# Attention and two expert layers in one kernel: scores in quarters of TensorE's array, a new order around the second product and the end of routing, and weight loads queued behind gathers

## The chip, the cores and the metric

The kernel runs on one core of one Trainium2 chip. The core has a matrix engine (TensorE, in the profile PE, with its weight loads PEld), a vector engine (VectorE, DVE), a scalar engine (ScalarE, ACT), a general engine (GpSimd, POOL) and a queue engine (SyncE, SP). Each runs its own instructions in the order in which they are written; semaphores tie them together. Working memory is SBUF; TensorE writes only into the accumulator memory PSUM. Transfers (DMAs) are started from the queues of SP, ACT and POOL and share 16 DMA engines. The metric is the device time of one execution in microseconds (us); less is better.

## The reference

Three layers in float32, each feeding the next. The sizes are 2 batches, 8 heads, 768 positions, head size 64, so 1536 tokens of width 512.

```
scores = q @ k.T / 8 - slope[head] * distance     # kept: the first 8 keys, and the 96 last ones
a = softmax(scores);  x = a @ v                   # attention, tokens x 512
xn = x / rms(x) * rms_g
x2 = (silu(xn @ w_gate) * (xn @ w_val)) @ w_out   # 512 -> 1536 -> 512
skip = x2 @ w_skip > 0 ; e = argmax(x2 @ w_route) # 8 experts
out = x2 ; out[skip] += gate * relu(x2 @ w1[e]) @ w2[e]    # 512 -> 1024 -> 512
```

The numbers of global and local keys are inputs: the fast path serves up to 32 and 97, and a general attention stands behind a branch for all other values. It is not taken with the data at hand.

## The kernel before

The program is one hand-ordered stream (no scheduler moves anything). It has five stages.

**Start.** Constants are made, a flag is computed from the two numbers and read by all engines, and each engine branches over the general attention (L962, `with tc.If(flag == 0)`). That body is written out in full: for each of two heads of a pair, six blocks of 128 queries, on TensorE 216 matmuls and transposes in all. Behind it `bias_tiles` makes the additive bias in four instructions of 576 columns on VectorE (L109).

**Attention** runs over 24 items: 8 pairs of heads by 3 groups of 256 queries, one item a step and five items in flight. In a step TensorE does the scores of item t (`qk`, L222), the transposes of the softmax of item t-2 (`trans`, L268) and the products with v of item t-3 (`pv`, L293); VectorE adds the bias and takes the row minimum (`ttr`, L233), scales (`norm`, L260), copies one half of the transposes out of PSUM (L277) and makes half of the next layer's input (L395); ScalarE does the exponentials (`exp`, L244), the other copy (L279) and the rest of the input (L393, L394). For the scores q is laid out on the host with zeros: 128 rows by 1536 columns a pair, in which each block of 128 columns holds 64 queries of head 0 in the upper 64 rows and the same 64 queries of head 1 in the lower ones, so that one matmul with full rows and columns gives both heads. A matmul in float32 shows as two matmuls in the trace, so the 4 of a step show as 8, and the 8 of `pv` (64 columns of the array each) as 16.

**First product** (`gemm1`, L517): 12 blocks of hidden units, the operands split into a high and a low float32r part, three matmuls for each product.

**Second product** (`gemm2`, L583): 12 tiles t of 128 tokens, 36 matmuls of 512 columns each. After the last one ScalarE scales the result into `x2` (L587). Inside tile t, at hooks (column, k): `turn(t-1)` at (0, 1) transposes x2 of the tile before on TensorE and copies it on ScalarE into `x2t` (L560); `routed(t-1)` at (0, 4) makes the routing logits from `x2t` (L568) and the expert choice; `slots(t-2)` at (0, 9) collects token numbers. Behind gemm2(t) stand `split_h(t+2)`, which makes the high and low parts of a coming tile in six casts on ScalarE (L546) and six subtractions on VectorE (L547), then some splits of expert weights (`split_next`, after tiles 1, 2, 5 and 6: 3, 2, 2 and 1 chunks; a cast on ScalarE, L824, and a subtraction on VectorE, L833, for each chunk of 512 KB), then loads (`load_next`: 4 after tile 6, 5 after tile 9, and 4 more inside tile 11).

**End of routing and experts.** The first expert's input x0 is gathered with selection matmuls (L1180) while the last tile's logits, ranks (L1223, L1224) and choice are made in turn between TensorE, ScalarE and VectorE. Then expert 0's first matmul group runs (`up`, L871), in it `gathers` computes the token lists and starts four indirect DMAs on POOL (L848), then `tx(1)` (transposes of expert 1's rows, L858), `th(0)` (transposes of the hidden layer, L890), and the loop over 9 jobs: `up`, `th`, `down` (L903), `put`. The 72 chunks of expert weights come in a fixed order, and a loaded chunk takes the place ("slot") of something used up, so the order in which slots come free sets when loads start.

```
        (0, 1): lambda: t >= 1 and turn(s, t - 1),
        (0, 4): lambda: t >= 1 and routed(t - 1),
        (0, 9): lambda: t >= 2 and slots(s, t - 2)})
    if t + 2 < 12:
        split_h(s, t + 2)
```

## Time and profile before

| | |
|---|---|
| median of 3 runs (lowest, highest) | 573.92 us (572.85, 575.16) |
| profiled execution, its own time | 574.41 us |
| its span, first to last instruction | 572.7 us |
| TensorE matmul busy | 532.6 us, 93% |
| VectorE, ScalarE, GpSimd busy | 401.0, 277.7, 135.0 us (70%, 48%, 24%) |
| mean granted TensorE clock | 0.981 |
| moved by DMA | 83.79 MB, mean 146 GB/s |

How to read it: the shares are means over five stages with different limits, so windows of the span are read stage by stage. A busy TensorE in a window says only that matmuls were in flight, since their ends are modelled; the distance between the starts of two groups is the safer measure. A row of the timeline is "start us, us, engine line operation out<-in xcount", and a bracket at its end is the idle time of the engine just before it with what ended it. PEldq, DVEq and so on are the engines' sequencers, which take branches and semaphores.

### The profile page before, as it was taken

What the parts mean: (1) busy time and instruction counts of PE and PEld (TensorE: products, weight loads), DVE (VectorE), ACT (ScalarE), POOL (GpSimd) and SP (SyncE); (2) the same over time, 40 slices, a digit from 0 to 9 for tenths busy, and PEclk for the clock granted to TensorE, in tenths of its full rate; (3) what the DMA queues carried; (4) which work ended last, traced back from release to release, by engine and by line L of the source; (5) the groups of instructions that cost most, each with busy time, mean ns of one, the idle gap of its engine ahead of it and who ended that gap; (6) DMA issues with size and microseconds to landing.
All of it is one profiled execution on the core that took longest, in us unless ns stands there. A gap on an engine that the chain in (4) does not pass through costs nothing. (4 is left out here: it accounts for less than half of the span.)

```text
span 572.7 us, 8709 instructions
## 1 busy us (share of the span) xinstructions
PE 532.6 (93%) x2932; PEld 444.9 (78%) x2932; DVE 401.0 (70%) x1014; ACT 277.7 (48%) x630; POOL 135.0 (24%) x132
## 2 busy tenths in 40 slices
PE   1899998899999999999999988989998799999994
PEld 1788887788888888888888867867888587878883
DVE  2888989557888688768864255545442299999971
ACT  0689889224323333323323444335231196988850
POOL 1445556011222222222212000000000201566201
PEclk9899999899999999999999988999999899999998
DMA  8645521021223323333206211106066899999000
GB/s 300 263 180 223 196 89 39 1 75 61 96 102 110 111 80 105 110 112 110 102 10 224 106 41 66 42 37 221 37 251 220 266 340 330 367 396 367 32 15 17
DMA packets 29511, 83.79 MB, mean 146 GB/s; under 512 B 3512, under 2 KB 3640, under 8 KB 29457
## 3 DMA queue, kind: packets, MB, share of 16 engines
q1 hardware_dynamic: 26064, 75.95, 36.7%
q0 software_dynamic: 1520, 4.03, 2.1%
q10 hardware_dynamic: 1872, 3.15, 1.5%
q8 instruction: 26, 0.43, 0.3%
q14 instruction: 29, 0.23, 0.1%
HBM read 75.42 MB, written 8.65 MB: 147 GB/s over the span
## 5 line engine op out<-in xcount | busy, mean ns | idle before, releaser
L517 PE MATMUL ps<-xh,wh 128*128 128x512 f32 (+1 forms) x304 | 115.9, 381 | 0.1
L517 PE MATMUL ps<-xh,wl 128*128 128x512 f32 (+1 forms) x304 | 115.3, 379 | 0.4 <-POOL wl L483 0.4
L517 PE MATMUL ps<-xl,wh 128*128 128x512 f32 (+1 forms) x304 | 115.2, 379 | 0.0
L833 DVE TENSOR_TENSOR ewl<-eraw,ewh 128x1024 fp32r<-128x1024 f32 x72 | 83.7, 1231 | 1.9 <-ACT ewh L824 1.7
L824 ACT CAST ewh<-eraw 128x1024 fp32r<-128x1024 f32 x72 | 71.3, 1057 | 7.0 <-DVE ewl L833 6.7
L517 PEld LDWEIGHTS ps<-xh,wl 128*128 128x128 f32 x304 | 57.3, 189 | 11.7 <-POOL wl L483 0.9
L517 PEld LDWEIGHTS ps<-xh,wh 128*128 128x128 f32 x304 | 57.4, 189 | 11.2 <-issue 0.8
L517 PEld LDWEIGHTS ps<-xl,wh 128*128 128x128 f32 x304 | 57.5, 189 | 10.6
L470 DVE SCALAR_TENSOR_TENSOR wraw<-f64t,wraw 128x512 f32<-128x512 f32 x36 | 44.0, 1221 | 28.8 <-ACT f64t L468 28.8
L583 PE MATMUL px<-woh,hh 128*128 128x512 f32 (+1 forms) x156 | 62.8, 403 | 0.0
L547 DVE TENSOR_TENSOR hl<-h,hh 128x256 fp32r<-128x256 f32 x72 | 25.5, 423 | 50.7 <-ACT hh L546 50.7
L583 PE MATMUL px<-wol,hh 128*128 128x512 f32 (+1 forms) x156 | 59.7, 383 | 0.0
L583 PE MATMUL px<-woh,hl 128*128 128x512 f32 (+1 forms) x156 | 59.6, 382 | 0.0
L483 POOL TENSOR_TENSOR wl<-f64t,wh 128x512 fp32r<-128x512 f32 x24 | 31.0, 1292 | 101.4 <-ACT wh L482 58.1
L222 PE MATMUL sc<-kd,qd 128*128 128x192 f32 (+1 forms) x192 | 39.0, 353 | 12.3 <-DVEq L962 12.3
L244 ACT ACTIVATE es<-es,m 128x192 f32<-128x192 f32 (+1 forms) x96 | 41.5, 435 | 17.3 <-DVE m L233 16.3
L482 ACT CAST wh<-f64t 128x512 fp32r<-128x512 f32 x24 | 14.9, 621 | 71.4 <-DVE f64t L480 71.4
L260 POOL TENSOR_SCALAR es<-es,z 128x192 f32<-128x192 f32 x46 | 35.6, 784 | 43.6 <-DVE z L253 17.4
L222 PEld LDWEIGHTS sc<-kd,qd 128*128 128x128 f32 x192 | 32.9, 211 | 15.2 <-PEq L962 12.3
L583 PEld LDWEIGHTS px<-woh,hl 128*128 128x128 f32 x156 | 30.2, 193 | 5.8
L583 PEld LDWEIGHTS px<-woh,hh 128*128 128x128 f32 x156 | 30.1, 193 | 5.3
L583 PEld LDWEIGHTS px<-wol,hh 128*128 128x128 f32 x156 | 30.2, 194 | 4.2
(192 smaller groups left out, 974.2 us busy)
## 6 DMA issues: line engine op xcount, KB each, us to landing
eraw<-in_w_dram SPq DMA_DIRECT2D x72, 512.0 KB, 6.5
wraw<-in_wgv_dram SPq DMA_DIRECT2D x24, 512.0 KB, 3.7
wraw<-in_w_out_dram SPq DMA_DIRECT2D x12, 512.0 KB, 3.2
vp<-in_vx_dram SPq DMA_DIRECT2D x8, 704.0 KB, 5.0
qd<-in_qx_dram SPq DMA_DIRECT2D x7, 768.0 KB, 5.6
kd<-in_kx_dram SPq DMA_DIRECT2D x7, 464.0 KB, 6.6
xm<-x SPq DMA_DIRECT2D x12, 256.0 KB, 2.6
out_dram<-x ACTq DMA_DIRECT2D x12, 256.0 KB, 2.9
```

The lines of the kernel that those rows point to most:

```text
L222: nc.tensor.matmul(sc[r][:, x, 0:n], lhsT=qs[pr][:, 2 * (2 * g + r) + x, :], rhs=ks[pr][:, k0:k0 + n], start=True, stop=True)
L244: nc.scalar.activation(e[:, r, x, e0:e0 + n], e[:, r, x, e0:e0 + n], AF.Exp, bias=m[:, j:j + 1], scale=-1.0, accum_out=z[:, j:j + 1])
L260: eng.tensor_scalar(e[:, r, x, e0:e0 + n], e[:, r, x, e0:e0 + n], z[:, j:j + 1], None, ALU.mult)
L470: nc.vector.scalar_tensor_tensor(out=a.bitcast(F32), in0=t, scalar=F64_LEAST, in1=a.bitcast(F32), op0=ALU.is_ge, op1=ALU.mult)
L482: nc.scalar.copy(hi, t)
L483: eng.tensor_tensor(lo, t, f(hi), ALU.subtract)
L517: nc.tensor.matmul(p, lhsT=w[:, k, :], rhs=x[c][:, k, a:b], start=n == 0, stop=n == 11)
L547: nc.vector.tensor_tensor(hl[:, i, :], src, f(hh[:, i, :]), ALU.subtract)
L583: nc.tensor.matmul(p, lhsT=h[:, k, :], rhs=w[k][:, c:c + N], start=n == 0, stop=n == 35)
L824: eng.copy(wh, raw)
L833: eng.tensor_tensor(wl, raw, f(wh), ALU.subtract)
```

## The change

**Scores.** q is no longer padded: 128 rows (64 of each head) by 768 columns a pair. A step's 4 score matmuls become 8, each with 64 rows and 64 columns of the array, in the order (head, chunk) = (0,0), (1,1), (0,1), (1,0). The chunk decides the PSUM tile, and for odd chunks the heads change halves, so that the slopes of the bias exist in two orders and each of the four bias instructions becomes four (16 in all, of 64 to 192 columns). `pv` reads its operand in a matching order. On TensorE, one step before (scores of one item, transposes, products; the two `sc` tiles are the PSUM tiles of the two blocks of 128 queries):

```order
L222 MATMUL sc_924<-kd,qd 128x192 x2
L222 MATMUL sc_925<-kd,qd 128x192 x2
L268 MATMUL pt<-ident,es_799 128x128 x8
L293 MATMUL po<-pts,vp 64x128 x8
L222 MATMUL sc_981<-kd,qd 128x192 x2
```

and the same step now (the two `sc` tiles are those of the two chunks):

```order
L240 MATMUL sc_518<-kd,qd 64x192
L240 MATMUL sc_519<-kd,qd 64x192 x2
L240 MATMUL sc_518<-kd,qd 64x192 x2
L240 MATMUL sc_519<-kd,qd 64x192 x2
L240 MATMUL sc_518<-kd,qd 64x192
L286 MATMUL pt<-ident,es_368 128x128 x8
L313 MATMUL po<-pts,vp 64x128 x8
```

Twice as many score matmuls stand in a step, each with half the rows and half the columns; the rest of the step is as it was.

**General attention** (not executed) runs its six blocks in a loop, so that the code over which the first branch leads is shorter: on VectorE 212 listed instructions before and 66 now, on TensorE 216 matmuls and transposes before and 36 now.

**Second product.** `split_h(t+1)` moves into the hook (0, 1), behind `turn(t-1)`; routing moves from (0, 4) to (0, 5), and the splits of expert weights and their loads follow it there, one tile later than before. On ScalarE, from the result of tile 1 to that of tile 2, before:

```order
L587 ACTIVATE x_3904<-px,r_1722 128x512
L590 DMA out_dram<-x_3904 128x512
L546 CAST hh<-h_795 128x256
L546 CAST hh<-h_2356 128x256
L546 CAST hh<-h_2357 128x256
L546 CAST hh<-h_2358 128x256
L546 CAST hh<-h_2359 128x256
L546 CAST hh<-h_2360 128x256
L824 CAST ewh<-eraw 128x1024 x3
L560 COPY x2t<-pxt 128x512
L656 ACTIVATE rex,rz<-lg,rm 128x8
L587 ACTIVATE x_4012<-px,r_1722 128x512
```

and now:

```order
L608 ACTIVATE x_3564<-px,r_1376 128x512
L611 DMA out_dram<-x_3564 128x512
L581 COPY x2t<-pxt 128x512
L567 CAST hh<-h_364 128x256
L567 CAST hh<-h_2030 128x256
L567 CAST hh<-h_2031 128x256
L567 CAST hh<-h_2032 128x256
L567 CAST hh<-h_2033 128x256
L567 CAST hh<-h_2034 128x256
L677 ACTIVATE rex,rz<-lg,rm 128x8
L845 CAST ewh<-eraw 128x1024 x3
L608 ACTIVATE x_3660<-px,r_1376 128x512
```

The copy `x2t`, for which the logits wait, goes from behind six casts and three weight casts to their front; the weight casts now stand ahead of the next result.

**End of routing.** Dummy matmuls (`keep`, into a PSUM tile `idle` that nobody reads) stand between the dependent steps; selection and gates of tile 10 move into tile 11; x0 is cast in two halves; expert 0's `th` goes ahead of expert 1's `tx`; the exponentials and ranks of tile 11 go behind the cast of x0. The loads of tile 11 are gone: 6 loads stand in tile 10 (5 after tile 9 before), and 8 are started from POOL's queue behind the four gathers. On POOL, before:

```order
L619 MEMSET ones_3824 128x128
L1134 MEMSET early 128x512
L1193 DMA early<-xm,si_f 128x512
L848 DMA exg<-xm,gi_s 128x512 x4
L913 DMA out_dram<-eo,si_s 1536x512
```

and now:

```order
L1222 DMA early<-xm,si_f 128x512
L869 DMA exg<-xm,gi_s 128x512 x4
L837 DMA eraw<-in_w_dram 128x2x512 x2
L837 DMA eraw<-in_w_dram 128x1024 x4
L837 DMA eraw<-in_w_dram 128x2x512 x2
L936 DMA out_dram<-eo,si_s 1536x512
```

Eight loads of 512 KB stand between the gathers and the first scatter of results, on a queue that had none of them.

```diff
@@ bias_tiles
+    spans = [(0, 64, 0), (64, 192, 4), (192, 384, 0), (384, 576, 4)]
     for hp in range(4):
-        nc.vector.scalar_tensor_tensor(out=s.bias[:, hp, :], in0=rel, scalar=slopes[:, hp:hp + 1],
-                                       in1=miss, op0=ALU.mult, op1=ALU.add)
+        for a, b, z in spans:
+            nc.vector.scalar_tensor_tensor(out=s.bias[:, hp, a:b], in0=rel[:, a:b],
+                                           scalar=slopes[:, z + hp:z + hp + 1],
+                                           in1=miss[:, a:b], op0=ALU.mult, op1=ALU.add)
@@ general_attention
-                for i in range(6):
+                with tc.For_i(0, 6, 1) as i:
...
@@ attention: load
-        qs[pr] = ap.tile([128, 12, 128], F32, name="qd", bufs=3)
+        q = qs[pr] = ap.tile([128, 768], F32, name="qd", bufs=3)
-        for a, b, c, d in ((0, 512, 0, 288), (512, 1536, 288, 928)):
+        for a, b, c, d in ((0, 256, 0, 288), (256, 768, 288, 928)):
@@ attention: qk
-            for x in range(2):
+            for h, x in ((0, 0), (1, 1), (0, 1), (1, 0)):
                 k0, _, _, n = part(g, r, x)
-                nc.tensor.matmul(sc[r][:, x, 0:n], lhsT=qs[pr][:, 2 * (2 * g + r) + x, :],
-                                 rhs=ks[pr][:, k0:k0 + n], start=True, stop=True)
+                d = slice(64 * h, 64 * h + 64)
+                o = slice(64 * (h ^ x), 64 * (h ^ x) + 64)
+                i = 128 * (2 * g + r) + 64 * x
+                nc.tensor.matmul(sc[x][o, r, 0:n], lhsT=qs[pr][d, i:i + 64],
+                                 rhs=ks[pr][d, k0:k0 + n], start=True, stop=True)
@@ attention: pv
-                                 rhs=pts[:, kt, :, o], start=kt == 0 or i == 0, stop=kt == 1)
+                                 rhs=blocks[:, kt, hh:4 - hh:3 - 2 * hh, :],
+                                 start=kt == 0 or i == 0, stop=kt == 1)
@@ Expert.tx
-        nc.scalar.copy(self.xh, xt)
+        for k in ((0, 2), (2, 4)) if x0 else ((0, 4),):
+            nc.scalar.copy(self.xh[:, k[0]:k[1], :], xt[:, k[0]:k[1], :])
@@ the loop over gemm2
-        gemm2(s, t, {
-            (0, 1): lambda: t >= 1 and turn(s, t - 1),
-            (0, 4): lambda: t >= 1 and routed(t - 1),
-            (0, 9): lambda: t >= 2 and slots(s, t - 2)})
-        if t + 2 < 12:
-            split_h(s, t + 2)
-        if t in (1, 5, 9):
-            for q in range(6):
-                s.slots.add(early if t < 9 and q == 0 else big, [f"h{t // 4}{q}"])
-        split_next({1: 3, 2: 2, 5: 2, 6: 1}.get(t, 0))
-        load_next({6: 4, 9: 5}.get(t, 0))
+        def one():
+            if t >= 1:
+                turn(s, t - 1)
+                split_h(s, t + 1)
+            if t in (2, 6, 10):
+                for q in range(6):
+                    s.slots.add(early if t < 10 and q == 0 else big, [f"h{t // 4}{q}"])
+                load_next({6: 0, 10: 6}.get(t, 0))
+        def two():
+            if t >= 1:
+                routed(t - 1)
+            split_next({2: 3, 3: 2, 6: 2, 7: 1}.get(t, 0))
+            load_next({7: 4}.get(t, 0))
+        gemm2(s, t, {(0, 1): one, (0, 5): two, (0, 9): lambda: t >= 2 and slots(s, t - 2)})
@@ inside and behind gemm2(11)
     def tenth():
...
+        run(select(s, 10), gates(s, 10))
     def adds():
...
-        load_next(4)
+    def keep(n):
+        w = experts[0].w[0][0]
+        for _ in range(n):
+            nc.tensor.matmul(idle, lhsT=w[:, 0:128], rhs=w[:, 512:1024], start=True, stop=True)
...
     logits(s, 11, range(2))
-    add(s.x2[10], first[10])
+    keep(1)
     turn(s, 11, 1)
+    add(s.x2[10], first[10], range(2))
     logits(s, 11, range(2, 4))
+    add(s.x2[10], first[10], range(2, 4))
...
     nc.tensor.matmul(rk0, lhsT=s.ones16, rhs=s.cum[:, 11, 0:1], start=True, stop=False)
+    keep(2)
     nc.tensor.matmul(rk0, lhsT=s.tri, rhs=oh0, start=False, stop=True)
     choose(11, rk0, oh0)
+    keep(2)
+    add(s.x2[11], first[11], stop=True)
+    keep(3)
     run(rest)
-    exps(s, 11)
-    add(s.x2[11], first[11], stop=True)
     free_wo(3, 6)
-    ranks(s, 11, s.ps_m, "misc")
...
     experts[0].tx(x0)
-    run(select(s, 10), select(s, 11))
+    exps(s, 11)
+    ranks(s, 11, s.ps_m, "misc")
+    run(select(s, 11))
     def gathers():
...
         for e in (1, 0, 2, 3):
             experts[e].gather()
+        load_next(8, nc.gpsimd)
...
+    experts[0].th()
     experts[1].tx()
-    experts[0].th()
```

## Rows read from the trace of the kernel before

**Rows 1.** Busy time by stretch of the span: the stretch and its length, then busy us (and instructions) of PE, PEld, DVE, ACT and POOL, the granted TensorE clock, the DMA engines' share and GB/s.

```profile
40.00:60.00 20.00, 20.00 (x187) 17.74 (x184) 18.07 (x88) 18.39 (x68) 10.99 (x14) 1.00 0.54 203
...
80.00:100.00 20.00, 18.23 (x174) 15.55 (x171) 19.45 (x78) 18.96 (x68) 11.52 (x13) 1.00 0.08 28
...
480.00:500.00 20.00, 20.00 (x99) 16.48 (x98) 20.00 (x21) 17.48 (x24) 8.37 (x3) 1.00 0.95 338
```

**Rows 2.** The instructions of line 962, the first branch: engine, operation, count, duration in ns (least, median, most), first and last start in us.

```profile
L962 ACTq COMPARE_BRANCH  x1: 50/50/50, 5.6 to 5.6; - x1
...
L962 PEldq COMPARE_BRANCH  x1: 6047/6047/6047, 5.7 to 5.7; - x1
...
L962 DVEq EVENT_SEMAPHORE  x1: 21/21/21, 12.2 to 12.2; - x1
```

**Rows 3.** Timeline of the start, all engines.

```profile
2.20 0.43 SPq L203 DMA_DIRECT2D kd<-in_kx_dram  x1
...
6.27 0.19 POOL L103 CAST slopes<-rel 128x4 f32<-128x4 f16 x1 [4.57 <-POOLq L962]
...
12.31 6.73 PE L222 MATMUL sc<-kd,qd 128*128 128x64 f32 x24 [12.31 <-DVEq L962]
...
14.44 0.82 DVE L109 SCALAR_TENSOR_TENSOR bias<-rel,slopes,miss 128x576 f32<-128x576 f16 x1
15.41 0.23 DVE L233 CUSTOM_DVE_ANT_0 es<-sc,bias 128x64 f32<-128x64 f32 x1 [0.15 <-DVE bias L109]
```

**Rows 4.** DMA issues of the first 40 us: KB of each and median us from issue to landing, for the first piece of k.

```profile
kd<-in_kx_dram SPq DMA_DIRECT2D x1, 144.0 KB, 3.9
```

**Rows 5.** Timeline of PE in steady attention: a score group, what follows it, and the second product and score group three steps on.

```profile
30.41 1.57 PE L222 MATMUL sc<-kd,qd 128*128 128x192 f32 x8
31.81 0.82 PE L268 MATMUL pt<-ident,es 128*128 128x128 f32 x6
...
39.03 1.15 PE L293 MATMUL po<-pts,vp 128*64 128x128 f32 x16
40.10 1.57 PE L222 MATMUL sc<-kd,qd 128*128 128x192 f32 x8
```

**Rows 6.** Timeline of PE over the second product, its plain matmuls left out: the rank matmul that opens each of tiles 2 to 8, and the logits of tile 1.

```profile
327.60 0.18 PE L678 MATMUL rk<-cum,ones 128*128 128x8 bf16 x1
...
334.23 1.06 PE L568 MATMUL lg<-w9t,x2t 128*128 128x9 f32 x8 [2.44 <-ACT x2t L560]
...
341.75 0.18 PE L678 MATMUL rk<-cum,ones 128*128 128x8 bf16 x1
...
354.97 0.18 PE L678 MATMUL rk<-cum,ones 128*128 128x8 bf16 x1
...
364.82 0.18 PE L678 MATMUL rk<-cum,ones 128*128 128x8 bf16 x1
...
374.69 0.18 PE L678 MATMUL rk<-cum,ones 128*128 128x8 bf16 x1
...
386.31 0.18 PE L678 MATMUL rk<-cum,ones 128*128 128x8 bf16 x1
...
397.02 0.18 PE L678 MATMUL rk<-cum,ones 128*128 128x8 bf16 x1
```

**Rows 7.** Timeline of ACT in tile 2 of the second product.

```profile
328.92 1.94 ACT L546 CAST hh<-h 128x256 fp32r<-128x256 f32 x6 [0.43 <-ACT x L587]
330.76 2.94 ACT L824 CAST ewh<-eraw 128x1024 fp32r<-128x1024 f32 x3
333.60 0.57 ACT L560 COPY x2t<-pxt 128x512 f32<-128x512 f32 x1
```

**Rows 8.** Timeline of PE from the end of the second product to the second expert.

```profile
439.29 0.51 PE L568 MATMUL lg<-w9t,x2t 128*128 128x9 f32 x4
...
445.19 1.22 PE L871 MATMUL eph<-ewh,exh 128*128 128x512 f32 x2 [0.73 <-ACT exh L861]
...
448.73 0.71 PE L871 MATMUL eph<-ewh,exh 128*128 128x512 f32 x2
...
456.67 0.63 PE L858 MATMUL ext<-ident,exg 128*128 128x128 f32 x4 [3.20 <-DMA exg<-xm,gi_s]
...
458.33 0.73 PE L871 MATMUL eph<-ewh,exh 128*128 128x512 f32 x2
```

**Rows 9.** Busy time by stretch, columns as in rows 1, at the first expert's start.

```profile
444.00:448.00 4.00, 3.27 (x12) 2.18 (x11) 1.82 (x10) 0.83 (x3) 0.00 (x0) 0.59 0.48 164
```

**Rows 10.** Timeline of POOL: the first of the four gathers, and a gather in the loop over the experts.

```profile
449.85 1.00 POOL L848 DMA_INDIRECT exg<-xm,gi_s  x1 [17.47 <-DVE rz L665]
...
502.62 6.16 POOL L848 DMA_INDIRECT exg<-xm,gi_s  x1 [0.30 <-issue]
```

**Rows 11.** Timeline of DVE around that second gather: subtractions with two operands in SBUF (L833), and one that reads PSUM (L862).

```profile
502.12 5.77 DVE L833 TENSOR_TENSOR ewl<-eraw,ewh 128x1024 fp32r<-128x1024 f32 x5
507.79 0.70 DVE L862 TENSOR_TENSOR exl<-ext,exh 128x512 fp32r<-128x512 f32 x1
508.39 3.50 DVE L833 TENSOR_TENSOR ewl<-eraw,ewh 128x1024 fp32r<-128x1024 f32 x3
```

**Rows 12.** DMA issues from 430 to 470 us: median us from issue to landing of the four gathers, and of the earlier gather of tiles 0 to 8.

```profile
exg<-xm,gi_s POOLq DMA_INDIRECT x4, 7.7
early<-xm,si_f POOLq DMA_INDIRECT x1, 3.4
```

More of the change, by code (lines that the diff above doesn't have):

```diff
@@ L147, in general_attention @@
                     for j in range(6):
-                        nc.tensor.matmul(sc[:, j, :], lhsT=q[:, 128 * i:128 * i + 128],
-                                         rhs=k[:, 160 * j:160 * j + 128], start=True, stop=True)
+                        nc.tensor.matmul(sc[:, j, :], lhsT=qi, rhs=k[:, 160 * j:160 * j + 128],
+                                         start=True, stop=True)
                     t = p.tile([128, 768], F32, name="gt")
@@ L217, in qk @@
         pr, g = it
-        sc = [s.ps_g.tile([128, 2, 256], F32, name=f"sc{r}", tag=f"ps{r}", bufs=2) for r in range(2)]
+        sc = [s.ps_g.tile([128, 2, 256], F32, name=f"sc{x}", tag=f"ps{x}", bufs=2) for x in range(2)]
         for r in range(2):
-            for x in range(2):
+            for h, x in ((0, 0), (1, 1), (0, 1), (1, 0)):
                 k0, _, _, n = part(g, r, x)
-                nc.tensor.matmul(sc[r][:, x, 0:n], lhsT=qs[pr][:, 2 * (2 * g + r) + x, :],
-                                 rhs=ks[pr][:, k0:k0 + n], start=True, stop=True)
+                d = slice(64 * h, 64 * h + 64)
[3 more added lines that the diff above has]
+                                 rhs=ks[pr][d, k0:k0 + n], start=True, stop=True)
         m = ap.tile([128, 4], F32, name="m", bufs=4)
@@ L233, in ttr @@
         nc.vector.tensor_tensor_reduce(
-            out=e[:, r, x, e0:e0 + n], in0=sc[r][:, x, 0:n], in1=s.bias[:, pr % 4, b0:b0 + n],
+            out=e[:, r, x, e0:e0 + n], in0=sc[x][:, r, 0:n], in1=s.bias[:, pr % 4, b0:b0 + n],
             scale=-0.125, scalar=3.0e38, op0=ALU.add, op1=ALU.min,
@@ L283, in pv @@
         pts = outs.pop((it, r))[1]
+        blocks = pts.rearrange("p k x (h c) -> p k (x h) c", c=64)
         if r == 0:
@@ L627, in route @@
 def route(s, t):
-    V, p = s.nc.vector, s.hpool
+    V, p = s.nc.vector, s.ixpool if t == 11 else s.hpool
     lg, skip = s.lg[t][:, 0:8], s.lg[t][:, 8:9]
@@ L854, in tx @@
         s, nc = self.s, self.s.nc
-        if xt is None:
+        x0 = xt is not None
+        if not x0:
             xt = s.ps_e.tile([128, 4, 128], F32, name="ext", bufs=1)
@@ L951, in attn_moe_kernel @@
     ints = load_ints(s)
-    s.rel = s.apool.tile([128, 1156], F16, name="rel", bufs=1)
+    s.rel = s.apool.tile([128, 1160], F16, name="rel", bufs=1)
     s.keep = s.apool.tile([128, 576], F16, name="keep", bufs=1)
-    s.slopes = s.apool.tile([128, 4], F32, name="slopes", bufs=1)
+    s.slopes = s.apool.tile([128, 8], F32, name="slopes", bufs=1)
     nc.sync.dma_start(s.rel, rel)
@@ L1251, in gathers @@
             experts[e].gather()
+        load_next(8, nc.gpsimd)
     experts[0].up(gathers)
-    run(gates(s, 10), gates(s, 11))
+    run(gates(s, 11))
     experts[0].relu()
@@ L1257, in attn_moe_kernel @@
         slots(s, t)
-    slt2 = s.ixpool.tile([24, 256], F32, name="slt2", bufs=1)
+    slt2 = s.ixpool.tile([24, 256], F32, name="slt2", tag="early", bufs=1)
     nc.vector.tensor_tensor(slt2, slt, s.sl, ALU.add)
+    experts[0].th()
     experts[1].tx()
-    experts[0].th()
     tab = s.ps_m.tile([128, 2, 24], F32, name="tab", tag="misc", bufs=1)
@@ L1323, in layout @@
     B, H, S, D = q.shape
-    qT = q.transpose(0, 1, 3, 2).reshape(B * H // 2, 2, D, S // 64, 64)
-    qx = np.zeros((B * H // 2, 2, D, S // 64, 2, 64), q.dtype)
-    for h in range(2):
-        qx[:, h, :, :, h, :] = qT[:, h]
+    qx = q.transpose(0, 1, 3, 2).reshape(B * H // 2, 2 * D, S)
     kT = k.transpose(0, 1, 3, 2).reshape(B * H // 2, 2 * D, S)
@@ L1336, in layout @@
     vx = v[:, :, np.stack(rows, axis=1), :].reshape(B * H // 2, 2, 128, 11, D).transpose(0, 2, 1, 3, 4)
[L1337 removed]
+    return qx, kT[:, :, cols], vx
 def relative():
```

33 lines of the change are left out of this document (21 added, 12 removed).

## The prediction

> **What bounds the kernel now.** One core at a mean clock of 0.981 leaves nothing to compare between cores, and the chain of waits comes down to the last scatter, so I read the span stage by stage: first the busy time by stretch, then the timelines of the edited places. In steady attention TensorE fills 20.00 of 20 us, with ScalarE at 18.39 and VectorE at 18.07 just below it; from 80 us VectorE (19.45) and ScalarE (18.96) are ahead of TensorE (18.23); over the experts TensorE and VectorE are both at 20.00 [rows 1]. So shorter scores pay in early and middle attention only, and expert time is not shortened at all. What else can be gained are waits: at the first branch, in tiles 2 to 5 of the second product, and between the first and second expert. I go through these four terms. The profiled execution took 574.41 us, 0.5 above the median of 573.92; the sum is made against the first.
>
> **Term 1, the start.** ScalarE's branch takes 50 ns at 5.6 us and GpSimd works at 6.27, but TensorE's branch takes 6047 ns, to 11.75, and VectorE's semaphore behind its own comes at 12.2 [rows 2, 3]. All read the same flag, so the difference is in what follows the branch. The two late engines are those with the long jumped-over bodies (216 matmuls and transposes on TensorE); after the change 36 are left. I take it that the code behind a short body is there at once, and the two start at about 6.3. They can't start sooner: the first k piece is issued at 2.20 and needs 3.9 to land, 6.1 [rows 3, 4]. Scores start at 12.31 now, so 6.0 comes free. Against it stand the bias pieces. An instruction of 576 columns takes 0.82 us, one of 64 columns (another operation, the nearest) 0.23 [rows 3]: 1.15 ns a column and 0.16 fixed, so three more starts cost up to 0.48 for each of four pairs, 1.9 in all; from 0.4 if starts overlap as back-to-back rows do there. I take 0.8, since VectorE has a tenth of its time free in steady attention. Term 1: 6.0 - 0.8 = **5.2** (3.5 to 6).
>
> **Term 2, scores in quarters.** The score group of a full step starts at 30.41, the transposes behind it at 31.81: 1.40 us for 8 matmuls of 192 columns with the whole array, 175 ns each. The 16 of the second product, half the array wide, go from 39.03 to 40.10: 1.07, 67 ns each for 128 columns [rows 5]. There will be 16 score matmuls a step, each a quarter of the array. No row shows a quarter, so bounds: one after the other, 16 x 175 = 2.80; two at a time at the second product's rate per column (0.52 ns x 192 = 100 ns), 1.60; four at a time 2.80/4 = 0.70. I take 1.07, the row nearest in kind (16 small matmuls that share the array), which says that starts, not columns, set the pace. That frees 0.33 a step. A pair is three steps, 30.41 to 40.10, 9.69 us; TensorE would need 9.69 - 3 x 0.33 = 8.7, but ScalarE at 18.39 of 20 needs 0.92 x 9.69 = 8.9, and with the waits between them I take 9.0: 0.7 a pair. About five of the eight pairs are bounded by TensorE, the late ones by VectorE and ScalarE [rows 1]: 5 x 0.7 = **3.5**. Ends: 5 if ScalarE reaches its 8.9 in six pairs and the start of the pipeline is shorter too; a loss of 24 x 0.2 = 4.8, less what the late pairs hide (a third), so 3.3, if only two run at a time.
>
> A change of mode between matmuls costs nothing that these rows show apart. The Trainium skill, "TensorEngine Tiling (Array Packing)", section Key Properties, says that TensorE is drained when the tiling mode changes, which speaks against this edit: a step now has three modes in place of two. By the rule, with both of the step's changes inside the second product's 1.07 us, and 128 columns at the higher clock being 53 ns (16 of them 0.85), one change is at most 0.11 to 0.22 and 24 more cost up to 2.6 to 5 us, an estimate; the 3.5 would fall to about 0 and the time to 554, inside the forecast's own range. The trace agrees only so far as that 0.22 leaves room for it.
>
> **Term 3, the second product.** The rank matmul that opens the routing of a tile comes once a tile. Undisturbed tiles are 9.85 and 9.87 long (354.97 to 364.82 to 374.69). From 327.60 to 341.75 it is 14.15, then 13.22 to 354.97, later 11.62 (374.69 to 386.31) and 10.71 (to 397.02): 4.3 + 3.4 + 1.8 + 0.8 = 10.3 above 9.86 [rows 6]. These are the tiles with expert weight splits. The mechanism is in ScalarE's queue: six casts (1.94) and three weight casts (2.94) run ahead of the copy x2t, which starts at 333.60 only [rows 7], and TensorE stands 2.44 us for it before the logits [rows 6]. The change puts x2t ahead of both. The casts behind it, 1.94 + 2.94, end some 5 us into a tile of 9.86, before the next x2 is due, and the subtractions on VectorE have the rest of the tile. What is late next is the weight casts against the next x2: they stand ahead of it, and I give 0.5 for the tiles where they brush it. Term 3: 10.3 - 0.5 = **9.8** (8 to 10.3; at 8 if the first of these tiles keeps half of its excess).
>
> **Term 4, the end of routing.** Expert 0's first group starts at 445.19 with a wait of 0.73, its next part at 448.73, the second expert's transposes at 456.67 after 3.20 of waiting for a gather, its first group at 458.33: 13.1 us from one to the other [rows 8]. Three parts: (a) TensorE's clock is 0.59 from 444 to 448 [rows 9], after a chain of short steps with gaps; in those 4.0 us it does what 0.59 x 4.0 = 2.4 would do, 1.6 lost; the dummy matmuls are to fill the gaps. (b) The wait of 3.20: the gathers took 7.7 us to land, the earlier one 3.4 [rows 12], and no loads of tile 11 are queued with them now, while th(0) goes into that time. (c) The start moves up some 0.6 since exponentials and ranks leave the path. 1.6 + 3.2 + 0.6 = 5.4; I take **4.6**, since the loads that expert 0's used chunks set free can still meet the gathers (2 to 5.6). The dummies themselves cost at most the end of one that overhangs its gap, 0.3.
>
> The loads on GpSimd: eight issues behind the gathers. A gather's issue takes 1.00 with 0.3 between [rows 10], so 8 x 1.3 = 10.4 us in which the queue is taken. Queued behind them are the first scatter and the fifth gather; both are needed only a job later (about 12 us), which hides it. The bound from above is the issue of 6.16 at 502.62 [rows 10]. There VectorE ran subtractions with two SBUF operands to 507.79, then one that reads PSUM; the issue ended at 508.78, though SBUF subtractions went on from 508.39 [rows 11]. So it was its start, with the read of the list, that was held, and a load without a list need not be. From below it is 0 (the cover holds), from above 8 x 6.2 - 10.4 = 39 of queue, of which two jobs of about 12 hide 24. I take 0, by the 1.00 row. The Trainium skill, "SBUF — State Buffer", on which engines contend, says that VectorE with two SBUF inputs holds up GpSimd work that reads SBUF; plain loads would be free of it, which agrees with 0, and the 6.16 row agrees with the rule.
>
> **Sum.** 5.2 + 3.5 + 9.8 + 4.6 = 23.1; 574.4 - 23.1 = 551.3, and on the median's side 550.8: **551**.
>
> **Rivals.**
> *Quarters one after the other* (slower). If the four quarters don't overlap, a score group is 16 x 175 = 2.80, 1.40 more a step; TensorE becomes the bound in all 24: +33.6, against 5.2 + 9.8 + 4.6 = 19.6 gained elsewhere: 588. It turns slower from 1.40 + 19.6/24 = 2.22 a step, 139 ns a matmul. Against it: the 16 of the second product, half as wide, already run at 67 ns [rows 5]. 4%.
> *Quarters two at a time.* 1.60 a step, term 2 is -3.3 for 3.5: 558. For it: the rate per column is what the half-array rows show. 15%.
> *The start stays.* If the branch waits for something other than the length of the body (a fetch at any jump, say), the change doesn't do what it says: 551 + 5.2 + 0.8 = 557. For it: no row shows what the 6047 ns are. Against it: 50 ns on ScalarE at the same branch. 12%.
> *GpSimd's loads are held.* If every issue took 6.16, 39 - 24 = 15 of queue would lie bare, the later chunks would land late and TensorE wait for them in jobs 1 and 2; as only issues that begin beside such a subtraction are held, I price a third of it, 5: 556. 9%.
> *The stall of the second product moves* to the next x2: half of term 3 back, 556. 3%.
> Forecast 57%.
>
> **How the numbers follow.** The forecast's own range is 546 to 555 (about half of each term's width, since they are independent). The range runs from 545 to 560, which takes in each rival but the first. A measurement of this kernel can tell about 0.5%, 2.9 us, from no change. All cases but the first are faster by more: 94%, with 2% for several together ending within 0.5%, and 4% slower.
>
> **What would show it.** VectorE and TensorE at work by about 6.3 to 6.5; score groups of 16 in about 1.07 and pairs some 9.0 apart; the second product's tiles all near 9.86 with x2t right behind the transposes; first groups of experts 0 and 1 about 9 us apart at a granted clock near 1.0; GpSimd's load issues near 1 us. Wrong would make it: a score group over 1.4, a branch still at 6 us, waits for x in the second product, or waits for chunks in jobs 1 and 2.

## The result

The changed kernel takes **554.33 us** (median of 4 runs, 554.07 to 554.68) against 574.33 for the kernel before (median of 4): ratio 0.9657, 95% interval [0.9641, 0.9673], so 19 to 21 us less. The forecast was 551, with a range from 545 to 560.

The same places of the program can be read off both traces. A "lead" is how much sooner the changed kernel gets there; its growth is what the stretch between two places gave.

| place | before, us | after, us | lead | gained on the way | forecast |
|---|---|---|---|---|---|
| first score matmul | 12.31 | 6.77 | 5.54 | 5.54 | 6.0 (term 1, ahead of the bias) |
| sixth score group | 30.41 | 25.33 | 5.08 | -0.46 | -0.8 (term 1, the bias pieces) |
| last score group | 92.83 | 85.62 | 7.21 | 2.13 | 3.5 (term 2) |
| first product starts | 104.91 | 99.14 | 5.77 | -1.44 | 0 |
| its last matmul | 309.61 | 303.05 | 6.56 | 0.79 | 0 |
| tenth rank matmul | 426.60 | 410.18 | 16.42 | 9.86 | 9.8 (term 3) |
| first expert starts | 445.19 | 428.72 | 16.47 | 0.05 | 0.6 (term 4c) |
| its next part starts | 448.73 | 430.96 | 17.77 | 1.30 | 1.6 (term 4a) |
| second expert starts | 458.33 | 438.38 | 19.95 | 2.18 | 3.2 (term 4b) |
| last scatter starts | 566.38 | 545.91 | 20.47 | 0.52 | |

Three of four terms came within 0.6 of their forecast: the first with 5.08 for 5.2, the third with 9.86 for 9.8, the fourth with 4.05 in all for 4.6 (5.4 for its parts, of which 4.6 was taken). The second, for which the scores were put into quarters, gave 2.13 from the sixth to the last score group, and 1.44 of it was lost again behind the last one. The rows, in order of the program:

**Start.** The instructions of the first branch in the changed kernel (engine, operation, count, duration in ns least/median/most, first and last start), which answer to [rows 2]:

```profile
L985 ACTq COMPARE_BRANCH  x1: 50/50/50, 5.9 to 5.9; - x1
...
L985 PEldq COMPARE_BRANCH  x1: 227/227/227, 6.0 to 6.0; - x1
L985 DVEq COMPARE_BRANCH  x1: 67/67/67, 6.0 to 6.0; - x1
...
L985 DVEq EVENT_SEMAPHORE  x1: 21/21/21, 6.6 to 6.6; - x1
```

and VectorE's branch in the kernel before:

```profile
L962 DVEq COMPARE_BRANCH  x1: 67/67/67, 5.7 to 5.7; - x1
```

TensorE's branch fell from 6047 ns to 227. VectorE's own branch takes 67 ns, and it took 67 before the change too: VectorE had not been late at its branch. In both kernels its semaphore comes last, 0.3 to 0.4 us behind TensorE's (6.3 and 6.6; 11.8 and 12.2), so it stood there until TensorE came. The bias of a pair of heads takes 1.21 us in four pieces for 0.82 in one, and by the sixth score group the lead is down to 5.08.

**Steady attention.** Timeline of TensorE over one pair, as in [rows 5]:

```profile
30.64 0.88 PE L240 MATMUL sc<-kd,qd 64*64 64x192 f32 x16
31.45 1.19 PE L286 MATMUL pt<-ident,es 128*128 128x128 f32 x8
...
38.53 0.93 PE L313 MATMUL po<-pts,vp 128*64 128x128 f32 x12
39.38 0.88 PE L240 MATMUL sc<-kd,qd 64*64 64x192 f32 x16
```

A score group now takes 0.81 us to the next group (31.45 - 30.64), 51 ns a matmul: four at a time, near the bound of 0.70, better than the 1.07 taken. The pair takes 8.74 where 9.0 was forecast and 9.69 stood [rows 5]. So far the step is better than its forecast. The busy times by stretch (columns as in [rows 1]) show where this ends:

```profile
40.00:60.00 20.00, 18.08 (x239) 12.81 (x232) 19.37 (x87) 18.37 (x70) 12.86 (x14) 1.00 0.52 178
60.00:80.00 20.00, 18.03 (x223) 13.90 (x221) 18.59 (x92) 17.35 (x62) 9.36 (x11) 1.00 0.27 92
```

From 40 to 60 us VectorE is at 19.37 of 20, and TensorE at 18. The pair that starts at 48.12 takes to 58.10, 9.98 us, longer than the 9.69 of [rows 5]. And behind the last score group stands a drain. Timeline of TensorE at the end of attention in the changed kernel:

```profile
85.62 0.88 PE L240 MATMUL sc<-kd,qd 64*64 64x192 f32 x16
...
90.09 0.66 PE L286 MATMUL pt<-ident,es 128*128 128x128 f32 x4 [1.68 <-DVE pts L295]
91.22 0.63 PE L286 MATMUL pt<-ident,es 128*128 128x128 f32 x4 [0.47 <-ACT pts L297]
...
95.51 1.97 PE L286 MATMUL pt<-ident,es 128*128 128x128 f32 x8 [2.33 <-DVE pts L295]
97.41 1.80 PE L313 MATMUL po<-pts,vp 128*64 128x128 f32 x16
99.14 0.50 PE L538 MATMUL ps<-xh,wh 128*128 128x512 f32 x1
```

and the two ends of the same stretch in the kernel before:

```profile
92.83 1.57 PE L222 MATMUL sc<-kd,qd 128*128 128x192 f32 x8
...
102.11 1.09 PE L268 MATMUL pt<-ident,es 128*128 128x128 f32 x8 [2.81 <-DVE pts L277]
...
104.91 0.80 PE L517 MATMUL ps<-xh,wh 128*128 128x512 f32 x1
```

At the last score group the lead is 7.21; the drain takes 13.52 in place of 12.08, and 5.77 is left. TensorE waits in it for VectorE's copies (1.68 and 2.33; before, 0.57 and 2.81), and the last transposes take 1.97 for 1.09, at a granted clock of 0.57 (92 to 100 us).

**Second product.** ScalarE in the tile in which it had run nine casts ahead of x2t [rows 7], and the rank matmuls that open the routing of tiles (as in [rows 6]):

```profile
323.25 0.59 ACT L581 COPY x2t<-pxt 128x512 f32<-128x512 f32 x1 [1.33 <-PE pxt L580]
323.73 1.94 ACT L567 CAST hh<-h 128x256 fp32r<-128x256 f32 x6
...
328.40 2.93 ACT L845 CAST ewh<-eraw 128x1024 fp32r<-128x1024 f32 x3
331.24 0.68 ACT L608 ACTIVATE x<-px,r 128x512 f32<-128x512 f32 x1
```

```profile
321.04 0.18 PE L699 MATMUL rk<-cum,ones 128*128 128x8 bf16 x1
...
330.95 0.18 PE L699 MATMUL rk<-cum,ones 128*128 128x8 bf16 x1
...
340.86 0.18 PE L699 MATMUL rk<-cum,ones 128*128 128x8 bf16 x1
```

x2t comes first, the weight casts end at 331.3, just as the next result is due, and the tiles are 9.91 and 9.91 long; all nine up to 410.18 are between 9.89 and 9.91.

**End of routing.** Timeline of TensorE, as in [rows 8], then GpSimd's queue, as in [rows 10]:

```profile
428.72 0.71 PE L894 MATMUL eph<-ewh,exh 128*128 128x512 f32 x2
...
430.96 0.72 PE L894 MATMUL eph<-ewh,exh 128*128 128x512 f32 x2
...
435.85 1.14 PE L913 MATMUL eht<-ident,eh 128*128 128x128 f32 x8
437.05 0.66 PE L880 MATMUL ext<-ident,exg 128*128 128x128 f32 x4
...
438.38 0.73 PE L894 MATMUL eph<-ewh,exh 128*128 128x512 f32 x2 [0.45 <-ACT exh L884]
```

```profile
432.07 1.00 POOL L869 DMA_INDIRECT exg<-xm,gi_s  x1 [16.07 <-DVE rz L686]
...
437.00 3.17 POOL L837 DMA_DIRECT2D eraw<-in_w_dram  x5
442.03 0.54 POOL L837 DMA_DIRECT2D eraw<-in_w_dram  x1 [1.87 <-DMA exg<-xm,gi_s]
444.40 0.72 POOL L837 DMA_DIRECT2D eraw<-in_w_dram  x1 [1.83 <-DMA exg<-xm,gi_s]
```

From expert to expert it is 9.66 us for 13.14, 3.48 less, in two parts. The first matmuls, up to the expert's next part, take 2.24 for 3.54 [rows 8], at a granted clock of 1.00 where 0.59 stood [rows 9]: 1.30. The other 2.18 come behind them. The wait of 3.20 for the gather is gone: the second expert's transposes start 5.0 us after the first gather's issue, 6.8 before [rows 8, 10], and th(0) fills the time. The eight loads on GpSimd take 0.54 to 0.80 each; the last four are issued while VectorE runs its weight subtractions without a break (439.35 to 448.5).

### The profile page after: what moved, and what is told of

Its sections match the earlier page's. It is cut to its first block, busy times and chain, and to the rows that moved or that the text cites. A ratio compares the mean times of both kernels' runs of the same rounds, so it can differ in the third digit from the quotient of the medians.

```text
span 552.3 us, 9096 instructions
## 1 busy us (share of the span) xinstructions
PE 524.2 (95%) x3132; PEld 425.8 (77%) x3132; DVE 404.8 (73%) x1026; ACT 277.5 (50%) x631; POOL 140.8 (25%) x140
## 5 line engine op out<-in xcount | busy, mean ns | idle before, releaser
L604 PE MATMUL px<-wol,hh 128*128 128x512 f32 (+1 forms) x156 | 58.2, 373 | 0.0
L262 ACT ACTIVATE es<-es,m 128x192 f32<-128x192 f32 (+1 forms) x96 | 41.4, 434 | 11.5 <-DVE m L251 10.3
L286 PE MATMUL pt<-ident,es 128*128 128x128 f32 x176 | 30.5, 305 | 10.1 <-DVE pts L295 6.6
L286 PEld LDWEIGHTS pt<-ident,es 128*128 128x128 f32 x176 | 20.7, 152 | 21.6 <-DVE pts L295 10.0
```

Source lines behind the costliest of these rows:

```text
L262: nc.scalar.activation(e[:, r, x, e0:e0 + n], e[:, r, x, e0:e0 + n], AF.Exp, bias=m[:, j:j + 1], scale=-1.0, accum_out=z[:, j:j + 1])
L286: nc.tensor.transpose(pt[:, kt, x, :], e[:, r, x, 128 * kt:128 * kt + 128], s.ident)
L604: nc.tensor.matmul(p, lhsT=h[:, k, :], rhs=w[k][:, c:c + N], start=n == 0, stop=n == 35)
```

## Experiments

Each edit is shown against the kernel named. Times are medians; ratios are to the kernel before on the same chip. *Loop*, *quarters* and *second* do one part of the change alone.

**Loop.** The kernel before, with the blocks of the general attention in a loop.

```diff
-                for i in range(6):
+                with tc.For_i(0, 6, 1) as i:
```

> The kernel before with the six blocks of the general attention in a loop, nothing else. If the wait at the first branch hangs on the length of the body that is jumped over: the branch on TensorE ends by about 6.5 us in place of 11.75, first scores at 6.3 to 6.8, and the time falls by 5.5 to 6.3 (about 568.4). If the branch waits for something else (rival), it still takes about 6 us and the time stays within 1 us of the kernel before.

569.33, ratio 0.9903 [0.9881, 0.9926]: 4.3 to 6.8 us less. TensorE's branch takes 233 ns, scores start at 6.52. The first theory holds. How much of the start's 5.8 reaches the end differs from execution to execution: in the profiled one, the slowest of four (571.57), the lead is 4.84 at the first product and 2.73 at the first expert.

**Quarters.** The kernel before, with plain q, scores in quarters and 16 bias instructions (the parts of the change's diff for bias_tiles, load, qk and pv).

```diff
+            for h, x in ((0, 0), (1, 1), (0, 1), (1, 0)):
+                nc.tensor.matmul(sc[x][o, r, 0:n], lhsT=qs[pr][d, i:i + 64],
+                                 rhs=ks[pr][d, k0:k0 + n], start=True, stop=True)
```

> The kernel before with scores in quarters (plain q, 16 bias instructions) and nothing else. Theory V, that attention as a whole is bounded by VectorE, whose work grows by 1.6 us for the bias: the score group falls from 1.40 to about 0.8 us on TensorE, but the start of the first product moves by less than 1 us either way and the time stays within 1.5 us of the kernel before. Theory T, that TensorE bounds five of eight pairs as the prediction had it: the first product starts 3 to 4 us sooner and the time falls by 3 to 4.

573.25, ratio 0.9983 [0.9962, 1.0004], which is not clear of no change. The score group falls to 0.81 us. From the first score to the first product it is 92.10 us (12.91 to 105.01) against 92.60 before. Theory V's numbers came out, theory T's did not: 0.5 us from some 13 of matmul time saved (24 steps at 0.5 to 0.6). How sure is the 0.5? *Loop* and *second* have the attention of the kernel before, and take 93.55 and 91.84, so a single profile is good to about 1 us here. The stretch from the sixth to the last score group is steadier: 62.43, 62.42 and 62.43 in these three, 60.31 in this run, and 60.27 to 60.48 in the changed kernel, *nokeep*, *sploads*, *noswap* and *third*. Quarters bring 2.1 there, and the ends of attention take it back.

**Second.** The kernel before, with the new order around the second product.

```diff
-            (0, 4): lambda: t >= 1 and routed(t - 1),
+        gemm2(s, t, {(0, 1): one, (0, 5): two, (0, 9): lambda: t >= 2 and slots(s, t - 2)})
-        if t + 2 < 12:
-            split_h(s, t + 2)
```

> The kernel before with the new order around the second product alone (split_h, routing, weight splits and loads moved; 5 loads in tile 10, 4 in tile 11 as before). If x2t behind the casts was the whole cause of the long tiles: all tiles 9.85 to 9.95, the first expert starts 9.5 to 10 us sooner, the time falls by 9.5 to 10.5 (about 564.3). If part of the stall moves to the next x2 (rival): a tile over 10.5 remains and the time falls by 5 or less.

563.07, ratio 0.9799 [0.9779, 0.9820]: 10.3 to 12.7 less. All tiles are 9.84 to 9.87 long; from the end of the first product to the first expert it is 125.84 us, 135.58 before: 9.74. The first theory holds. The time fell somewhat more than the 9.74 of that stretch; the profiled execution was also 1.25 ahead when the first product ended, in a part of the program that the edit doesn't touch.

**Diagonal.** The changed kernel, without the swap of heads for odd chunks, so that only two of the four quarters are in use, and with four bias instructions.

```diff
-                o = slice(64 * (h ^ x), 64 * (h ^ x) + 64)
+                o = d
```

> The changed kernel, but with the heads not swapped for odd chunks: each head's scores stay in its own half of columns, so only the two diagonal quarters of the array are used, and the bias is again four instructions of 576 columns (1.6 us less for VectorE). Score group by the rate of the second product per column: 1.4 to 1.6 us against 0.81 of the changed kernel; if neighbours in one quarter run strictly one after the other, no two at once, 2.8. Theory V: the time stays within 1 us of the changed kernel (554.3), since TensorE has room for 0.6 a step and VectorE gets 1.6 back. Theory T: the time rises by 3 to 5.

557.56 (554.10 to 558.99), ratio 0.9687 [0.9639, 0.9734]: wide, and by time not apart from the changed kernel. The trace is plainer: a score group takes 1.45 us (90 ns a matmul, somewhat less than the 100 ns that the rate per column of the products with v gave for two at a time), a pair 9.89, and the first product starts at 103.28, 4.1 later than in the changed kernel. TensorE is busy for 20.00 of 20 us from 40 to 60 and from 60 to 80: it is the bound again, and theory T's numbers came out for this kernel. So neither theory is the whole: two at a time TensorE decides, four at a time it does not.

**Poolnorm.** The changed kernel, with one more scaling of a step on GpSimd.

```diff
-            norm(b, 0, 1, nc.vector)
+            norm(b, 0, 1, nc.gpsimd if t < n else nc.vector)
```

> The changed kernel, with one of the two remaining scalings by 1/z of a step moved from VectorE to GpSimd (24 instructions of 0.28 to 0.35 us off VectorE, 24 of 0.8 onto GpSimd, which is busy 10 to 13 of 20 us there). Theory V, that VectorE bounds attention as a whole now: pairs after the fifth become shorter, the first product starts 2 to 4 us sooner than at 99.14, the time is 550 to 552. Theory T, that the loss lies with TensorE's own tail and clock: no change within 1 us. Rival G: GpSimd, at some 2.4 of 2.95 us a step, becomes late itself and the step grows: 556 or more.

**550.14**, ratio 0.9576 [0.9556, 0.9596], clear of the changed kernel's interval. The first product starts 3.0 us sooner:

```profile
84.38 0.88 PE L240 MATMUL sc<-kd,qd 64*64 64x192 f32 x16
...
96.15 0.80 PE L538 MATMUL ps<-xh,wh 128*128 128x512 f32 x1
```

VectorE has some 7 us less to do (24 scalings of about 0.3), and TensorE's work is the same. Theory V's numbers came out, but not its place: the late pairs did not become shorter. From the sixth to the last score group it is 61.02 us for 60.30. TensorE still waits there for VectorE's copies (0.97 and 0.75), and now for GpSimd's scalings too (0.27 twice). The gain lies at the two ends: 16.55 for 18.56 up to the sixth score group, 11.77 for 13.52 behind the last.

**Oldnorm.** The same one-line edit on the kernel before.

> The kernel before with one scaling by 1/z of a step moved from VectorE to GpSimd and nothing else. If TensorE bounds the steps of the kernel before (as the prediction had it): the spacing of its score groups stays at 9.7 a pair and the first product starts less than 1.5 us sooner. If VectorE bounded attention there already: the first product starts some 3 us sooner, as it did when the same edit was made to the changed kernel.

569.44, ratio 0.9928 [0.9903, 0.9954]. From the first score to the first product it is 88.59 us against 92.60, yet the score groups in the middle stay 9.70 a pair (29.61, 39.31, 49.01, 58.70). Both theories are half right: the steady steps were TensorE's, as the prediction had it, and the 4.0 us came from the two ends. To the sixth score group it is 16.29 for 18.10 (1.8), the drain behind the last is 9.51 for 12.08 (2.6), and 0.4 was lost between. Only the drain is the edit's for certain: *second*, which lacks it, takes 16.46 to its sixth score group, at a granted clock of 1.00 from 24 to 28 us, where the kernel before has 0.61; its drain takes 12.95, and that of *loop* 12.45.

**Quartersnorm.** The kernel before, with both edits, quarters and scaling.

> The kernel before with scores in quarters and the scaling on GpSimd, both. Theory that TensorE and VectorE are two bounds close together: what the two edits bring together is more than the sum of what each brings alone (quarters alone about 1 us); the first product starts about 4 us sooner than before, and the time is about 570. Theory that they add up: quarters 1 plus whatever the scaling alone brings.

569.24, ratio 0.9919 [0.9895, 0.9943]: by time the same as the scaling alone. From the first score to the first product it is 87.10 us, 1.5 less than with the scaling alone (88.59). Quarters bring 0.5 without the relief and 1.5 with it, a difference that is within what profiles of one attention differ by. In the steady stretch from the sixth to the last score group they bring the same in both: 2.1 without (62.43 to 60.31), 2.2 with it (62.79 to 60.60). So the two edits add up there, and taking VectorE's load off doesn't give the rest of the 3.5 back. ScalarE is busy for 17.94 of 18 us from 30 to 48; that it is the next bound is not shown.

**Nokeep.** The changed kernel without its eight dummy matmuls.

```diff
-        for _ in range(n):
+        for _ in range(0):
             nc.tensor.matmul(idle, lhsT=w[:, 0:128], rhs=w[:, 512:1024], start=True, stop=True)
```

> The changed kernel without the eight dummy matmuls. If they are what holds the clock: the granted clock falls in the stretch about the first expert's start (below 0.8 for some 4 us, 0.59 in the kernel before), the first expert's first groups run at half speed and the first group of the second expert comes 1 to 2 us later: 555.5 to 556.5. Rival: the reordered steps alone leave no gap worth a fall, the clock stays at 1.00 and the time within 0.7 of 554.3, or below it by what the dummies take.

554.60, ratio 0.9658 [0.9637, 0.9678]: the same. The busy times by stretch at the first expert's start, the changed kernel first, then this one:

```profile
425.00:429.00 4.00, 3.94 (x26) 2.94 (x26) 2.00 (x10) 0.65 (x2) 0.00 (x0) 1.00 0.21 79
```

```profile
425.00:429.00 4.00, 3.14 (x26) 2.60 (x24) 1.63 (x9) 0.73 (x3) 0.00 (x0) 1.00 0.35 131
```

The clock is 1.00 in both. Without the dummies the first expert starts 0.76 sooner, counted from the end of the first product (124.91 for 125.67). The rival holds: in this run the reordered steps alone keep the clock up, and up to the first expert the dummies cost 0.76 and give nothing (125.67 in all seven profiles that have them). At the last scatter 0.5 of it is left (242.38 us from the end of the first product, for 242.86), too little to show in the times.

**Sploads.** The changed kernel, with the eight loads on SP's queue.

```diff
-        load_next(8, nc.gpsimd)
+        load_next(8)
```

> The changed kernel with the eight loads behind the gathers started from SP's queue in place of GpSimd's, at the same point of the program. Prediction's claim that GpSimd's queue costs nothing: same within 1 us, and the gathers land at about the same time. Rival 1: loads on SP start before the gathers and compete with them, so that the wait of TensorE for the second expert's rows returns (up to 3.2 us): 555 to 558. Rival 2: on GpSimd the loads were held up (they took 10 us from the first to the last issue), and SP brings the chunks sooner: 552 to 553.

555.91 (553.70 to 556.75), ratio 0.9666 [0.9635, 0.9697]. SP starts its loads at 425.05, eight us ahead of the first gather (433.08); TensorE then waits:

```profile
439.66 0.66 PE L880 MATMUL ext<-ident,exg 128*128 128x128 f32 x4 [1.66 <-DMA exg<-xm,gi_s]
```

From the first expert's start to the second's it is 11.27 us for 9.66. From the end of the first product to the last scatter it is 244.83 us, 242.86 in the changed kernel: 2.0 lost, as rival 1 had it, though the times alone don't settle it. (Four other kernels with the changed kernel's end, *third*, *diagonal*, *poolnorm* and *best*, take 242.80 to 243.57.)

**Noswap.** The changed kernel, with the second expert's transposes ahead again.

```diff
-    experts[0].th()
     experts[1].tx()
+    experts[0].th()
```

> The changed kernel with the second expert's transposes ahead of the first expert's hidden-layer transposes, as before the change. In the changed kernel the hidden-layer transposes took 1.14 us and the next step waited 0.1 for the gather; so without the swap TensorE waits about 1.3 us for the gather and the time rises by 0.6 to 1.3 (555 to 555.6). Rival: TensorE's time is not the bound there, since VectorE is full from 439 us on and its first weight splits don't wait for this: no change within 0.5.

555.13, ratio 0.9666 [0.9645, 0.9686]. The same stretch takes 243.90, 1.04 more, the amount expected, of which 0.29 stands between the first and the second expert; the medians are 0.8 apart.

**Third.** The changed kernel, with three blocks written out in each turn of the loop.

```diff
-                with tc.For_i(0, 6, 1) as i:
+                with tc.For_i(0, 6, 3) as i3:
+                  for z3 in range(3):
+                    i = i3 + z3
```

> The changed kernel with three of the six blocks of the general attention written out in each turn of its loop: 108 matmuls and transposes on TensorE in the body that is jumped over, against 36 in the changed kernel and 216 before. If the wait at the branch grows with the length of the body: TensorE's branch ends about 3 us later than in the changed kernel, first scores at 9 to 10 us. If there is a length up to which the code behind the branch is there at once: first scores at 6.8 still, or at 12 if this body is past it.

The instructions of the first branch in this kernel:

```profile
L985 PEldq COMPARE_BRANCH  x1: 227/227/227, 6.2 to 6.2; - x1
```

227 ns with 108 matmuls and transposes in the body, as with 36; 6047 with 216. It isn't a price per instruction: if the length decides, there is one between 108 and 216 from which the branch has to wait. The bodies of 36 and 108 also have the inner loop, which the one of 216 lacks, and no run takes length and loop apart. (554.71 us, one run.)

**Best.** Poolnorm, with the bias's pieces reordered on the host so that those of one slope are neighbours: 8 instructions in place of 16.

```diff
-    s.kinds = [0, 64, 192, 384]
+    s.kinds = [0, 256, 64, 384]
-    spans = [(0, 64, 0), (64, 192, 4), (192, 384, 0), (384, 576, 4)]
+    spans = [(0, 256, 0), (256, 576, 4)]
```

> The changed kernel with the scaling on GpSimd, and with the bias laid out so that pieces with the same slopes are neighbours: 8 bias instructions in place of 16 (8 starts of about 0.16 us less for VectorE). If VectorE still bounds part of attention: 0.5 to 1.3 us below the 550.1 of the scaling alone. If ScalarE or GpSimd bounds it by now: the same as that within 0.5.

**549.96** (549.31 to 550.81), ratio 0.9579 [0.9553, 0.9605]: the same as poolnorm by time. From the first score to the first product it is 88.56 us against 89.35; one profile each doesn't make that a gain. With poolnorm it is the fastest version here, some 4 us under the changed kernel.

## Why the prediction was right or wrong

**Term 1 held** (5.54 for the 6.0 of the start, 5.08 for 5.2 with the bias), and *loop* shows that the jumped-over body is the cause. Two details were wrong. VectorE was not an engine with a long branch of its own; it waited for TensorE. And the wait doesn't grow with the body, as *third* shows. The rival "the start stays" fell with both runs. Whether the body's length or its loop decides, and what the branch waits for, is not shown. The bias's 0.46 for 0.8 is one profile's difference, in a stretch in which *second* and *loop*, with one and the same attention, differ by 2.2.

**Term 2 failed, by size** (2.13 for 3.5, and 0.69 with what the drain took back), at the step "about five of the eight pairs are bounded by TensorE: 5 x 0.7". The price of a quarter was taken too high, not too low (0.81 for 1.07), and the pair's 9.0 came out as 8.74. But only the pairs up to 48 us got shorter: the lead grows from 5.08 at the sixth score group to 7.93 at the fourteenth, and then falls to 7.21. From there VectorE, which I had read as "just below" TensorE at 18.07 of 20, fills 19.37. The next bound was computed for a pair in isolation, from the share in one window, while VectorE's and ScalarE's work comes unevenly: it is heaviest where 80 to 100 us already showed 19.45 and 18.96 [rows 1]. What TensorE gained became waits, mostly for VectorE's and ScalarE's copies. That VectorE's load is what holds the late pairs is not shown: with one scaling moved away, VectorE fell from 19.37 to 18.45 of 20 and they were no shorter (*poolnorm* 61.02 for 60.30). Which step of the chain between the engines sets their pace stays open.

Part of the gain was given back in the drain, which I had not listed as a place at all: 13.52 for 12.08, and 13.44 to 13.76 in the six kernels with quarters and without the moved scaling that run four at a time, against 12.08 to 12.95 in three with the old attention. Of the 1.44, 0.9 is the last transposes at a lower clock (1.97 for 1.09). That part is not the quarters' own, since *second*, with the old attention, has it too, at a granted clock of 0.60 from 100 to 104 us:

```profile
100.80 1.97 PE L268 MATMUL pt<-ident,es 128*128 128x128 f32 x8 [2.81 <-DVE pts L277]
```

*Poolnorm*, *oldnorm* and *quartersnorm* show that the drain hangs on VectorE (11.77, 9.51 and 9.96). They don't show that it hangs on VectorE's load. In the drain of every kernel without the moved scaling, before and after the change, VectorE stands still three times beside a GpSimd operation (1.28, 1.41 and 1.86 us for 0.32, 0.17 and 0.32; the rows are at the end); in the four with it, once (1.86). The other two are worth 2.2 us, of 1.75, 2.57 and 3.48 that the drain gained. So the edit may help there as much by the order on GpSimd that it changes, and no run takes the two apart.

The rivals to this term fell: quarters one after the other (2.80 a group) and two at a time (1.60) against 0.81. At 1.45, *diagonal* is near two at a time. On the rule that TensorE is drained at a change of tiling mode (the Trainium skill, "TensorEngine Tiling (Array Packing)", Key Properties): a group's 0.81 leaves 0.11 above the four-way bound of 0.70, within the estimate of 0.11 to 0.22, so no run contradicts it; it decided nothing here, since the group came out below the 1.07 that was taken.

**Term 3 held** (9.86 for 9.8) with its mechanism; *second* alone shows it. I gave 0.5 for weight casts that brush the next result. They end at 331.3 against a result begun at 331.24, but in *second* the tiles with weight casts are no longer than the others (9.84 to 9.87). The changed kernel's 9.89 to 9.91 stand in all tiles alike, some 0.4 in nine, and no run says why.

**Term 4 nearly held** (4.05 for 4.6, of which 0.52 came behind the second expert), with every part smaller than forecast. (a) The clock is back at 1.00 at the first expert, worth 1.30 for 1.6, but not by the dummies: it is at 1.00 without them (*nokeep*), and with them (c) came to 0.05 for 0.6. Their price "at most 0.3" should have been 0.8. (b) The wait for the gather is gone, worth 2.18 for 3.2. Undoing the place of the loads costs 1.6 of it (*sploads*; 2.0 by the last scatter), undoing the swap 0.3 (*noswap*; 1.0 by the last scatter), by one profile each.

**The loads on GpSimd** cost nothing that shows, as taken: 0.54 to 0.80 an issue, at most 0.72 for the four beside VectorE's subtractions, far from 6.2, so that rival fell. More than that, they are useful: the queue holds them behind the gathers, which SP's queue doesn't do.

**The first product's 0.79** was in no term. In the kernel before its first matmuls run at 0.80 and 0.63 us before they settle at 0.39, in the changed one at 0.50; *poolnorm*, which starts it at 0.80 again, needs 204.61 us for it, as the kernel before (204.70), not 203.91. *Nokeep* and *sploads*, which are the changed kernel up to there, start it at the lower clock as well and need 204.87 and 204.83. It comes and goes with the clock at the end of attention, not with the change.

## What to carry to other kernels

When two engines are at 20.0 and 18.1 of 20 us, speeding up the first is worth a tenth at most, and less where the second's work is uneven (62.4 us became 60.3 here); read its busiest window and the drain at the stage's end, where one moved line did more than the whole new score layout. Before a gain of 1 us in a stretch is put down to an edit, see how far that stretch differs between kernels that have the same program there. A copy that others wait for belongs ahead of bulk casts on an in-order queue. A queue's order can be used as a gate: loads put behind gathers on the same queue can't overtake them.

## What the runs showed of the hardware

Jumping over a long body can cost 6 us at a branch on TensorE, all at once: 227 to 233 ns over bodies of 36 and 108 matmuls and transposes with an inner loop, 6047 to 6443 in the five kernels with 216 written out.

VectorE's short scalings stand still beside a GpSimd operation with two operands, and hardly beside one with one operand. Timelines of the changed kernel in the drain, VectorE, then GpSimd:

```profile
87.59 1.28 DVE L278 TENSOR_SCALAR es<-es,z 128x192 f32<-128x192 f32 x1
...
90.63 1.41 DVE L267 TENSOR_SCALAR z<-z 128x4 f32<-128x4 f32 x1 [0.21 <-ACT es L262]
```

```profile
87.48 1.27 POOL L504 TENSOR_TENSOR wl<-f64t,wh 128x512 fp32r<-128x512 f32 x1 [2.22 <-DVE es L278]
...
90.21 1.81 POOL L422 TENSOR_TENSOR sq<-sq 128x768 f32<-128x768 f32 x1
```

and the second of these on VectorE in *poolnorm*, where GpSimd's sum comes later:

```profile
88.35 0.17 DVE L267 TENSOR_SCALAR z<-z 128x4 f32<-128x4 f32 x1 [0.60 <-ACT es L262]
```

An addition on 128x4 that else takes 0.17 us took 1.41 and ended at 92.04, when GpSimd's sum ended (92.02). All five such operations on `z` and `es` that began beside a two-operand one in attention (0.94 to 1.86 us long, the fifth at 92.53) ended within 0.12 of it. Of the 22 beside GpSimd's one-operand scalings none took over 0.36; in the kernel before, four of 22 took 0.45 to 0.51. The Trainium skill, "SBUF — State Buffer", Who interferes with whom, says that of a VectorE operation in a two-port mode and a GpSimd operation the later one is blocked for the whole of the other; the five agree with it, the 22 don't show it, and no run shows which mode these operations run in. Moving those sums away from VectorE's path was not tried by itself.
